# Attention feeding a max-out layer: eleven equal score groups per head pair, the attention remainder through a padded 128-row tile, a first K in two parts, and weights requested at the start in chunks

## The chip, the cores and the metric

One core of one Trainium2 chip runs the kernel. The metric is device time in microseconds (us) for one execution, of which medians over several executions are quoted. Single executions of one kernel mostly lie within 1% of each other. The profiled execution is one of them; its span (the time inside the core) is shorter than its device time by 1.7 to 1.9 us. The profiled execution of the kernel before was one of its slower ones (417.6 us).

The engines are named as in the profile: PE is the matrix engine and PEld its weight loads, ACT the scalar engine (here the exponentials), DVE the vector engine, POOL the general engine (here it sums Q and converts K and V), SP issues the transfers. Line numbers such as L412 are those of the kernel in question, so the same line has different numbers in different kernels.

## The reference

```python
# q, k, v: [8 batches, 8 heads, 1152 rows, 64], float32
q_pool = mean of each two neighbouring rows of q            # 576 rows
attn   = softmax(q_pool @ k.T / 8)                          # per batch and head
x      = (attn @ v), heads side by side                     # 4608 tokens x 512
out    = maximum(x @ w1, x @ w2) @ w_out                    # w1, w2: 512x1024, w_out: 1024x512
```

Both kernels use max(a, b) = b + relu(a - b). With `wd = w1 - w2` and `w21 = w2 @ w_out`, the output is `x @ w21 + relu(x @ wd) @ w_out`. Below, **W** is the work on PE that prepares `w21` (transposes of w2 and 32 matmuls), **H** is `relu(x @ wd)`, and **P** is the last product, in tiles of up to 128 tokens with 12 matmuls each (4 from `x @ w21`, 8 from H). H and P together are called the MoE work here.

## The kernel before

A small planner runs while the kernel is built. It keeps an estimated clock for each engine and puts every instruction into that engine's list. The lists go into the kernel in that order, with semaphores between the engines. So whatever the planner puts first is also waited for first, even where it is late on the chip.

The work goes by head pair: 32 pairs, four to a batch. For one pair PE makes score groups into three PSUM buffers (`sps`), ACT takes the exponential of each group, and PE multiplies them with V (**AV**), with a column of ones that gives the softmax sum. Everything on PE other than scores shares two PSUM accumulators (`fb`, "lanes"). When four pairs are done, the 576 tokens of a batch exist, are transposed into `xT`, and H and P can run on them. They fill the time in which PE would wait for ACT.

```python
NA, NB = 512, 64                    # 576 pooled queries = 512 + 64
# 9 score groups of 2 x 512 columns (eta), then the 64-column rests of all key tiles:
# one group of 8 rests and one of a single rest (etb)
pe_cost  = [0.22] * NT + [0.24, 0.04]
act_cost = [0.953] * (NT + 1) + [0.21]
BURST = 3                           # up to three score groups behind each other
...
def rest():                         # the AV remainder: both heads' 64 queries as one 128-row tile
    for t in range(NT):
        e.matmul(fb[m][:, 4*66:4*66+131], etb[es][:, t, :, :]..., vE[vs][:, t, :, :]...[:, 0:131], ...)
...
W_AT = (0, 1, 3)                    # w2 is requested at pair 0, w_out at pair 1, w1 at pair 3,
def w_load(part):                   # each as one transfer of 2 MB
    ...
def xtrans(b):                      # x is transposed by five DMA transposes, for every batch
    ...
# start: Q0 summed on POOL, K0 loaded in one piece and converted on DVE
load_q(0); load_k(0); cast_k(0); cast_q(0)
```

The softmax here doesn't subtract the row's maximum and nothing guards it: scores larger than these inputs give would overflow.

Of the kernel before, what the change touches and what calls it, by code (L numbers as in the profile page):

```python
# [9 lines left out]
EXP = mybir.ActivationFunctionType.Exp  # L10
ALU = mybir.AluOpType


class Plan:
# [38 lines left out]
    def op(self, eng, fn, r=(), w=(), dma=None, cost=0.1, mode="f", after=(), solo=False):  # L53
        n = len(self.ops)
        deps, raw = self.deps(r, w, after)
# [95 lines left out]
def bass_funnel_attn__then__act_maxout2_kernel(  # L151
# [14 lines left out]
    QP = 64  # L166
    QU = SQ // QP
    NA = 512
    NB = SQ - NA
    NCH = NA // P  # L170
# [5 lines left out]
    NBLK = NTOK // 512  # L176
    assert D == 64 and S == NT * P and SQ == QP * QU and QU == NT and C == H * D and E == 512
    assert NB == 64 and NTOK % 512 == 0 and NT == 9
    scale = 0.5 / float(D) ** 0.5

    ctx = ExitStack()
    with ctx:
# [10 lines left out]
        qp = [sbuf([QP, QU, 2, D], BF16, f"qp{s}") for s in range(2)]  # L193
# [4 lines left out]
        eta = [sbuf([P, 2, NT, NA], BF16, f"eta{s}") for s in range(2)]  # L198
        etb = [sbuf([P, NT, 2, NB], BF16, f"etb{s}") for s in range(2)]
        rc = [sbuf([P, 6], FP32, f"rc{s}") for s in range(2)]  # L200
# [13 lines left out]
        osb = [stage[:, NC_ * F + s * E:NC_ * F + (s + 1) * E] for s in range(3)]  # L214
# [6 lines left out]

        def setup():
            def ones(g):
                for s in range(3):
                    last = g.memset(vE[s][:, :, :, 64:66], 1.0)
                return last

            op("POOL", ones, w=["vE0", "vE1", "vE2"])
            op("POOL", lambda g: g.memset(ident[:, :], 1.0), w=["id0"])
            op("POOL", lambda g: g.affine_select(  # L230
                ident[:, :], ident[:, :], pattern=[[1, P]], compare_op=ALU.is_equal,
                fill=0.0, base=0, channel_multiplier=-1), r=["id0"], w=["ident"])

        def load_k(i):
            b, h0, s = i // NHP, 2 * (i % NHP), i % 3
            op("SP", lambda e: e.dma_start(
                kraw[s][:, :, :, :].rearrange("p h t d -> p h (t d)"),
                k[b, h0:h0 + 2, :, :].rearrange("h (p t) d -> p h (t d)", t=NT)),
                w=[f"kraw{s}"], dma=f"d_k{s}", cost=1.7)

        def load_q(i):
# [3 lines left out]
                q[b, h0:h0 + 2, :, :].rearrange("h (p r) d -> (h p) (r d)", p=QP)),  # L245
# [9 lines left out]
        def cast_k(i):  # L255
            s, r = i % 2, i % 3
            op("DVE" if i == 0 else "POOL", lambda g: g.tensor_scalar(  # L257
                kbf[s][:, :, :, :].rearrange("p t h d -> p h t d"), kraw[r][:, :, :, :],
                1.0, 1.0, ALU.mult, ALU.mult), r=[f"kraw{r}"], w=[f"kbf{s}"], cost=1.13)

        def ktrans(i):
# [4 lines left out]
                r=[f"kbf{s}"], w=[f"kT{v3}"], dma=f"d_kT{v3}", cost=1.5, mode="t")  # L266

        def cast_q(i):
            s, r = i % 2, i % 3
            for half in range(2):  # L270
                a = qraw[r][half * QP:half * QP + QP, :, :, :]
                op("POOL", lambda g, half=half, a=a: g.tensor_tensor(  # L272
                    qp[s][:, :, half, :], a[:, :, 0, :], a[:, :, 1, :], ALU.add),
                    r=[f"qraw{r}"], w=[f"qp{s}.{half}"], cost=1.4,
                    solo=half == 1)
# [16 lines left out]
        def qtrans(i):  # L292
            s = i % 2

            def go(e, m):
                mb = fb[m][:, :].bitcast(BF16)
                for u in range(QU):
                    last = e.transpose(  # L298
                        mb[:, u * QP:(u + 1) * QP],
                        qp[s][:, u, :, :].rearrange("p h d -> p (h d)"), ident[0:QP, 0:QP])  # L300
# [8 lines left out]
        def ktrans_pe(i):  # L309
# [3 lines left out]
            for lo, hi in ((0, 5), (5, NT)):  # L313
# [8 lines left out]
                def evac(m, lo=lo, hi=hi):  # L322
# [4 lines left out]
                        [f"f{m}"], [f"kT{v3}", f"f{m}"], 0.7)  # L327
                jobs.append(Job("q", [unit([f"kbf{s}", "ident"], 0.055 * (hi - lo), go)], evac,
                                ("k", i) if lo else None))
            return jobs  # L330

        def av_jobs(i):
# [4 lines left out]
            c0 = h0 * D  # L337

            def chunk(half, sb):
                def go(e, m):  # L340
                    for t in range(NT):
                        last = e.matmul(  # L342
                            fb[m][:, sb * 66:sb * 66 + 65],
                            eta[es][:, half, t, sb * P:(sb + 1) * P],
                            vE[vs][:, t, half, 0:65],
                            start=(t == 0), stop=(t == NT - 1))
                    return last
                return unit([f"eta{es}.{t}" for t in range(NT)] + [f"vE{vs}"], 0.275, go)

            def rest():  # L350
                def go(e, m):
                    for t in range(NT):
                        last = e.matmul(  # L353
                            fb[m][:, 4 * 66:4 * 66 + 131],
                            etb[es][:, t, :, :].rearrange("p h c -> p (h c)"),
                            vE[vs][:, t, :, :].rearrange("p h c -> p (h c)")[:, 0:131],
                            start=(t == 0), stop=(t == NT - 1))
                    return last
                return unit([f"etb{es}.{NT}", f"etb{es}.{NT + 1}", f"vE{vs}"], 0.53, go)

            def norm(half):
                def evac(m):
                    n = 6 if half == 0 else 4
                    c = c0 + half * D
                    a = fb[m]
                    dve(lambda e: e.reciprocal(  # L366
                        rc[half][:, 0:n],
                        a[:, 0:n * 66].rearrange("p (j c) -> p j c", c=66)[:, :, 64:65]),
                        [f"f{m}"], [f"rc{half}"], 0.13)
                    dve(lambda e: e.tensor_tensor(  # L370
                        xnat[xs][:, 0:NCH, c:c + D],
                        a[:, 0:NCH * 66].rearrange("p (j c) -> p j c", c=66)[:, :, 0:D],
                        rc[half][:, 0:NCH].unsqueeze(2).to_broadcast([P, NCH, D]),
                        ALU.mult),
                        [f"f{m}", f"rc{half}"],
                        [f"xn{xs}.{j}.{h0 + half}" for j in range(NCH)]
                        + ([f"f{m}"] if half else []), 0.38)
                    if half == 0:
                        dve(lambda e: e.tensor_scalar_mul(
                            xnat[xs][0:64, NCH, c:c + D], a[0:64, 264:264 + D],  # L380
                            rc[0][0:64, 4:5]), [f"f{m}", "rc0"], [f"xn{xs}.{NCH}.{h0}"], 0.2)
                        dve(lambda e: e.tensor_scalar_mul(  # L382
                            xnat[xs][0:64, NCH, c + D:c + 2 * D], a[64:P, 330:330 + D],
                            rc[0][64:P, 5:6]), [f"f{m}", "rc0"],
                            [f"xn{xs}.{NCH}.{h0 + 1}", f"f{m}"], 0.2)
                return evac

            last = ("x", b) if i % NHP == NHP - 1 else None
            return [
                Job("a", [chunk(0, sb) for sb in range(NCH)] + [rest()], norm(0)),  # L390
                Job("a", [chunk(1, sb) for sb in range(NCH)], norm(1), last)]
        gcount = [0]

        def scores(i, g):
# [4 lines left out]
            gcount[0] += 1  # L399

            def one(e, half, t, lo, n, col):
                h = half * 64
                return e.matmul(  # L403
# [505 lines left out]
```

## Time and profile before

| | before |
|---|---|
| device time, median | 415.4 us (414.8 to 416.0, 4 executions) |
| first exponential starts / last one ends | 13.1 / 341.7 us |
| first H matmul / first P matmul | 83.3 / 101.0 us |
| PE busy / ACT busy | 91% / 76% |

Parts 1, 2 and 4 of the page of the kernel before: busy time, the span in 40 slices of 10.4 us (tenths busy; PEclk is the granted clock of PE), and the chain of work that ended last.

```profile
PE 379.6 (91%) x4846; PEld 203.6 (49%) x4905; DVE 156.3 (38%) x355; ACT 314.4 (76%) x370; POOL 164.9 (40%) x136
PE   0787897899999999999999999999999999999996
ACT  1788997899989997999799999999999980011121
PEclk9988998999999999999999999999999999999999
PE 80%; DVE 8%; ACT 6%; issue 2%; DMA 1%; POOL 1%; another core or an unknown queue 0%
```

PE is the engine to save: it is busy nearly all the time from the ninth slice on, and it holds 80% of the chain. ACT is not full in mid-kernel; its weak stretches are at the start, and after 342 us it has almost nothing to do.

The two groups of exponentials and the two groups of AV matmuls, from the list of groups, with busy time and the mean length of one in ns; and from the list of waits (us in total, times, longest) the line for ACT.

```profile
L415 ACT ACTIVATE eta<-sps 128x1024 bf16<-128x1024 f32 x288 | 269.6, 1047 | 35.0 <-PE sps L403 34.3
L427 ACT ACTIVATE etb<-sps 128x1024 bf16<-128x1024 f32 x64 | 38.8, 673 | 0.2
L342 PE MATMUL fb<-vE,eta 128*128 128x65 bf16 x2304 | 88.7, 194 | 6.1 <-DVE xnat L382 3.1
L353 PE MATMUL fb<-vE,etb 128*128 128x131 bf16 x288 | 23.1, 226 | 0.0
ACT eta L415 <- PE sps L403: 34.3, 31, 11.1
```

A mean of 194 ns for a 65-column matmul is not what it costs PE: the records overlap (2304 of 194 ns would be 447 us, and the busy time is 88.7), and in the trace their starts are 29 ns apart.

PE's time can be split with prices that are read from such starts: 216 ns for 512 columns, 29 ns for 65, and 94 ns extra whenever a matmul on 64 rows follows one on 128 (312 ns instead of 216 to the next start) or the reverse (309 ns). What remains of the span is waiting (what matmuls take longer at a granted clock of 0.50 is in it too: there the 65-column starts are 55 ns apart).

| kernel before, us | pure PE work | changes of height | waits | waits 0 to 85 / 85 to 340 / after 340 us |
|---|---|---|---|---|
| span 415.9 | 333.8 | 321 x 0.094 = 30.2 | 51.9 | 32.6 / 10.5 / 8.7 |

So the 52 us of waits are what a better order could win, and 33 of them lie before 85 us, where the MoE work has not begun. Four lines of the timeline show what comes before it: the four subtractions `w1 - w2`, the last normalisation of the first batch's tokens, their five transposes by DMA, and the first H matmul. The columns are start, length, engine, line, operation.

```profile
63.41 6.53 DVE L488 TENSOR_TENSOR wd<-stage,xT 128x1024 bf16<-128x1024 f32 x4
70.06 0.42 DVE L370 TENSOR_TENSOR xnat<-fb,rc 128x256 bf16<-128x256 f32 x1
70.51 7.90 SPq L446 DMA_TRANSPOSE xT<-xnat  x5
83.28 0.92 PE L549 MATMUL fb<-xT,wd 128*128 128x448 bf16 x4
```

### The profile page before, as it was taken

The numbers are of one execution on the slowest core, as the hardware profiler recorded it, in microseconds if no ns is written. First come the engines' busy times: TensorE is split into PE (matmuls) and PEld (weight loads), VectorE is DVE, ScalarE is ACT, GpSimd is POOL, SyncE is SP. The second block draws the span as 40 slices with busy tenths as digits, with TensorE's granted clock in tenths as the row PEclk, the third lists the DMA queues.
The fourth block names the chain that finished last, engine by engine and source line by source line (L and its number), as shares of the span: only waits on it lengthen the run. The fifth ranks groups of instructions, "written<-read, shape, count | busy, mean of one in ns | idle before, by whom it ended". The sixth has DMA issues, their size and how long they took to land.

```text
span 415.9 us, 11123 instructions
## 1 busy us (share of the span) xinstructions
PE 379.6 (91%) x4846; PEld 203.6 (49%) x4905; DVE 156.3 (38%) x355; ACT 314.4 (76%) x370; POOL 164.9 (40%) x136
## 2 busy tenths in 40 slices
PE   0787897899999999999999999999999999999996
PEld 0355544545365536545555545555555554344442
DVE  1224738344233533244334433344333444432210
ACT  1788997899989997999799999999999980011121
POOL 5982643654346534644165536452751000000000
PEclk9988998999999999999999999999999999999999
DMA  8999997796499949974999899849964203423223
GB/s 297 403 401 391 401 283 182 155 333 159 78 344 249 277 91 315 328 225 59 303 283 240 131 307 305 267 64 325 296 138 93 46 2 65 96 50 76 64 61 66
DMA packets 81600, 85.76 MB, mean 206 GB/s; under 512 B 54416, under 2 KB 54416, under 8 KB 81552
## 3 DMA queue, kind: packets, MB, share of 16 engines
q1 hardware_dynamic: 81552, 85.05, 74.0%
q8 instruction: 38, 0.62, 0.6%
q14 instruction: 10, 0.08, 0.1%
HBM read 62.91 MB, written 9.44 MB: 174 GB/s over the span
## 4 chain that ended last, share of the span: by engine, by line
PE 80%; DVE 8%; ACT 6%; issue 2%; DMA 1%; POOL 1%; another core or an unknown queue 0%
PE fb L581 23%; PE fb L342 17%; PE sps L403 17%; PE fb L549 15%; ACT eta L415 5%; PE fb L353 4%; PE fb L298 2%; DVE wd L488 2%; PE fb L516 1%; DVE stage L598 1%; DMA qraw<-in_q_dram 1%; DVE xnat L370 1%; DVE xnat L382 1%; DVE wo L483 1%; POOL qp L272 1%
## 5 line engine op out<-in xcount | busy, mean ns | idle before, releaser
L415 ACT ACTIVATE eta<-sps 128x1024 bf16<-128x1024 f32 x288 | 269.6, 1047 | 35.0 <-PE sps L403 34.3
L272 POOL TENSOR_TENSOR qp<-qraw 64x576 bf16<-64x576 f32 x64 | 90.8, 1419 | 60.9 <-PE fb L298 54.2
L403 PE MATMUL sps<-qpT,kT 64*128 64x64 bf16 (+1 forms) x1152 | 104.6, 290 | 7.3 <-ACT eta L415 5.5
L342 PEld LDWEIGHTS fb<-vE,eta 128*128 128x128 bf16 x2304 | 79.4, 98 | 37.3 <-issue 14.4
L342 PE MATMUL fb<-vE,eta 128*128 128x65 bf16 x2304 | 88.7, 194 | 6.1 <-DVE xnat L382 3.1
L549 PE MATMUL fb<-xT,wd 128*128 128x512 bf16 (+2 forms) x304 | 76.3, 358 | 3.1 <-issue 1.3
L581 PE MATMUL fb<-wo,stage 128*128 128x512 bf16 (+1 forms) x275 | 76.5, 380 | 1.7 <-issue 1.0
L564 DVE TENSOR_SCALAR stage<-fb 128x512 bf16<-128x512 f32 (+2 forms) x68 | 44.4, 656 | 69.4 <-PE fb L549 69.0
L403 PEld LDWEIGHTS sps<-qpT,kT 64*128 64x128 bf16 x1152 | 31.2, 94 | 54.2 <-ACT eta L415 27.6
L279 POOL TENSOR_SCALAR vE<-vraw 128x1152 bf16<-128x1152 f32 x32 | 37.3, 1165 | 47.7 <-issue 35.0
L257 POOL TENSOR_SCALAR kbf<-kraw 128x1152 bf16<-128x1152 f32 x31 | 36.7, 1184 | 48.0 <-DMA kT<-kbf 47.3
L366 DVE RECIPROCAL rc<-fb 128x6 f32<-128x6 f32 x64 | 12.1, 189 | 114.0 <-PE fb L353 71.7
L549 PEld LDWEIGHTS fb<-xT,wd 128*128 128x128 bf16 x320 | 25.3, 97 | 37.2 <-DVE stage L564 6.0
L558 ACT ACTIVATE stage<-fb 128x288 bf16<-128x288 f32 (+1 forms) x12 | 5.7, 473 | 50.0 <-PE fb L549 50.0
L581 PEld LDWEIGHTS fb<-wo,stage 128*128 128x128 bf16 (+1 forms) x296 | 26.0, 98 | 30.3 <-issue 7.4
L581 PE MATMUL fb<-w,xT 128*128 128x512 bf16 (+1 forms) x130 | 37.3, 381 | 3.3 <-DVE stage L598 1.4
L427 ACT ACTIVATE etb<-sps 128x1024 bf16<-128x1024 f32 x64 | 38.8, 673 | 0.2
L598 DVE COPY stage<-fb 128x512 f32<-128x512 f32 (+1 forms) x32 | 22.1, 690 | 31.4 <-PE fb L581 31.1
L370 DVE TENSOR_TENSOR xnat<-fb,rc 128x256 bf16<-128x256 f32 x64 | 27.2, 424 | 2.2
L353 PE MATMUL fb<-vE,etb 128*128 128x131 bf16 x288 | 23.1, 226 | 0.0
L298 PE MATMUL fb<-ident,qp 64*128 64x64 bf16 x288 | 14.0, 192 | 9.8 <-POOL qp L272 8.8
L298 PEld LDWEIGHTS fb<-ident,qp 64*128 64x128 bf16 x288 | 10.7, 96 | 19.6 <-POOL qp L272 8.8
(27 smaller groups left out, 113.7 us busy)
## 6 DMA issues: line engine op xcount, KB each, us to landing
qraw<-in_q_dram SPq DMA_DIRECT2D x32, 576.0 KB, 7.0
kraw<-in_k_dram SPq DMA_DIRECT2D x32, 576.0 KB, 5.9
vraw<-in_v_dram SPq DMA_DIRECT2D x32, 576.0 KB, 8.1
out_dram<-stage SPq DMA_DIRECT2D x72, 128.0 KB, 2.5
xT<-in_moe_w_dram SPq DMA_DIRECT2D x1, 2048.0 KB, 15.6
stage<-in_moe_w_out_dram SPq DMA_DIRECT2D x1, 2048.0 KB, 19.3
stage<-in_moe_w_dram SPq DMA_DIRECT2D x1, 2048.0 KB, 17.4
xT<-xnat SPq DMA_TRANSPOSE x40, 2.5
```

The lines of the kernel that those rows point to most:

```text
L257: op("DVE" if i == 0 else "POOL", lambda g: g.tensor_scalar(kbf[s][:, :, :, :].rearrange("p t h d -> p h t d"), kraw[r][:, :, :, :], 1.0, ...
L272: op("POOL", lambda g, half=half, a=a: g.tensor_tensor(qp[s][:, :, half, :], a[:, :, 0, :], a[:, :, 1, :], ALU.add), r=[f"qraw{r}"], w=[f" ...
L279: op("POOL", lambda g: g.tensor_scalar(vE[r][:, :, :, 0:D].rearrange("p t h d -> p h t d"), vraw[r][:, :, :, :], 1.0, 1.0, ALU.mult, ALU.m ...
L298: last = e.transpose(mb[:, u * QP:(u + 1) * QP], qp[s][:, u, :, :].rearrange("p h d -> p (h d)"), ident[0:QP, 0:QP])
L342: last = e.matmul(fb[m][:, sb * 66:sb * 66 + 65], eta[es][:, half, t, sb * P:(sb + 1) * P], vE[vs][:, t, half, 0:65], start=(t == 0), stop ...
L353: last = e.matmul(fb[m][:, 4 * 66:4 * 66 + 131], etb[es][:, t, :, :].rearrange("p h c -> p (h c)"), vE[vs][:, t, :, :].rearrange("p h c -> ...
L403: return e.matmul(sps[r][:, half, col:col + n], kT[ks][h:h + 64, t, :], qpT[qs][h:h + 64, lo:lo + n], start=True, stop=True)
L415: return e.activation(eta[es][:, :, g, :], sps[r][:, :, :], EXP, scale=scale)
L427: return e.activation(etb[es][:, t0:t0 + n, :, :].rearrange("p t h c -> p h t c"), sps[r][:, :, 0:n * NB].rearrange("p h (t c) -> p h t c" ...
L549: last = e.matmul(fb[m][:, 0:size], wd[:, ct, ft * P:(ft + 1) * P], xT[:, ct, n0:n1], start=(ct == 0), stop=(ct == NC_ - 1))
L564: dve(lambda e: e.tensor_scalar_max(gT[:, ft, g0:g0 + size], fb[m][:, 0:size], 0.0), [f"f{m}"], [f"gT.{g0 // 64}.{ft}", f"f{m}"], 0.1 + si ...
L581: last = e.matmul(fb[m][0:hi - lo, :], lhs, rhs, start=(j == 0), stop=(j == NC_ + NF - 1))
```

## The change

Its intent: bring the start of the exponentials and of the MoE work forward, and make the score groups uniform so that bursts of three always fit. Cut to its core:

```diff
-    NA = 512
-    NB = SQ - NA
+    NG = 11
+    cut = [(NT * SQ * g // NG + 1) // 2 * 2 for g in range(NG + 1)]     # 11 groups of 942 +- 2 columns
...
-        eta = [... [P, 2, NT, NA] ...]; etb = [... [P, NT, 2, NB] ...]
+        et = [sbuf([P, 2 * NT * SQ + HP], BF16, f"et{s}") for s in range(2)]   # one tile, 64 zero columns behind
...
-                            eta[es][:, half, t, sb * P:(sb + 1) * P],
+                        a = (half * NT + t) * SQ + sb * P           # sb = 0..4: the fifth tile reads
+                            fb[m][:, sb * 66:sb * 66 + 65], et[es][:, a:a + P],   # 64 columns too far
-            def rest(): ...                                        # 131-column remainder
-                    if half == 0: (two more tensor_scalar_mul for the remainder)
+                        xnat[xs][:, :, c:c + D], a[:, :, 0:D], ...  # normalisation: one 128x320 operation
...
+        def xtrans_pe(b): ...           # x of the first and the last batch transposed on PE, copied by DVE
+        X_PE = (0, B - 1)
...
-            part 0: one dma_start of 2 MB per weight array; w_cast waits for the whole array
+            for c in range(NC_): dma_start of 512 KB each; each cast waits for its own chunk
...
-            if i in W_AT: w_load(W_AT.index(i)) ...                 # pairs 0, 1, 3
...
-        load_q(0)
-        load_k(0)
-        cast_k(0)                       # DVE
-        cast_q(0)                       # POOL
+        load_k(0, 0, 3)
+        load_q(0)
+        load_k(0, 3, NT)
+        cast_k0(0, 3, "kraw0.0")        # ACT
+        cast_q(0)                       # DVE
+        cast_k0(3, NT, "kraw0")         # ACT
         load_k(1); load_q(1); load_v(0); start_k(1); cast_q(1); cast_v(0)
+        start_w(0)                      # w2, in front of K2 and Q2
         load_k(2); load_q(2); load_v(1)
+        start_w(1)                      # w1
         load_k(3); load_q(3); load_v(2)
+        start_w(2)                      # w_out
```

Further: PE units are one matmul instead of two, either lane takes any job, the planner chooses by fixed ranks of the kinds of work and no longer by how far ACT is ahead, the output is 36 tiles of 128 rows instead of 37, and there are four output buffers instead of three.

## The prediction

> **What bounds it now.** TensorE. The page shows PE 91% busy against ACT 76%; the chain of waits that ended last is 80% PE. ACT does not bind in mid-kernel: its exponentials start every 904 ns back to back (timeline), which would give about 294 us for 32 head pairs; they take 329 us (13.1 to 341.7 us) and idle 34 us waiting for score matmuls (waits). After 342 us only MoE matmuls run, about 70 us.
>
> Starts of successive matmuls in the trace give a price per PE item: 216 ns for 512 columns, 29 ns for the 65-column AV matmul, 60 ns for the 131-column AV remainder, 220 ns for a score pair on two 64-row halves. Each change between 64-row and 128-row matmuls adds about 94 ns (312 instead of 216 going in). [...] At these prices the PE work is some 332 us plus 30 of changes; the other 54 us are PE waits: about 34 before 85 us (weights arrive late; the first MoE matmul is at 84.8 us), 16 in mid-kernel, 5 in the tail.
>
> **What the change does.**
> - AV remainder: 9 x 60 = 540 ns becomes 18 x 29 = 522 ns per pair. Neutral on PE. DVE normalisation falls from four operations after the first half (about 1.2 us) to two (about 0.7 us).
> - Uniform groups: same columns and the same 11 exponentials. From 1047 ns for 1024 columns and 301 for 128, 942 cost about 980, about 836 apart: 9.2 us a pair, as now. Neutral. But bursts can be three groups nearly always (now about 2.4 by my count of changes): about 250 changes instead of 320, about -6 us.
> - Output tiles: 36 of 128 rows instead of 37: 12 x 216 ns = -2.6 us. PE transposes of x for first and last batch: +2.2 us, but they replace about 6 us of DMA transposes in front of the last blocks.
> - Startup: K0's first third is loaded first, Q0 summed on DVE (estimate 1.3 to 1.9 us) instead of POOL (3.4 us), K0 cast on ACT. First exponential at about 9.5 us instead of 13.1: -3.5 us, all on the chain.
> - Weights requested at once, in chunks: landed by about 35 us (12.8 MB at the traced 400 GB/s) rather than after 60. MoE can start when batch 0 is transposed, about 58 us instead of 85. This moves PE work into idle time: early waits fall from 34 to about 20 us, 3.5 of it the startup counted above.
> - Single-matmul units, either lane for any job: mid-kernel waits 16 to perhaps 12 us.
>
> Sum: -6 -0.5 -14 -4 = about -24 us, nearly all on the chain.
>
> **Predicted 393 us**, range 383 to 405. Faster by over 2%: 0.92; within 2%: 0.07; slower: 0.01.
>
> **What would show it right.** First exponential near 9.5 us; first MoE matmul near 58 us; exponentials end near 320 to 330 us; changes of matmul height near 250; exponential duration near 980 ns; the normalisation near 0.5 us for 128x320; ACT idle behind score matmuls well below 34 us.
>
> **What would make it wrong.** Early weight traffic could delay K/Q/V of pairs 2 and 3 (DMA is saturated to 40 us), so ACT would starve. Bursts of three need three free score buffers and may leave ACT dry. Running 8 hidden-layer jobs in a row with two PSUM buffers may expose their 0.69 us DVE copy, so that tail waits grow.

The 30 us of changes are the traced 94 ns times about 320. For two numbers the traces say more than the text: two sums of 576 columns, at the 1.21 (shortest) to 1.69 us (mean) of the subtractions on DVE in the kernel before (1024 columns), make 1.36 to 1.90 us, and Q0's two, on DVE in the kernel after, took 0.75 us each (5.11 to 6.63 us); and "saturated" stands for 297 to 403 GB/s up to 42 us, with the DMA engines busy for 80% or more (the page's digits 8999).

## More of the kernel before

`wd` is ready at 69.9 us, and the tokens' transposes are issued at 70.5 to 78.4 us. Both come before H at 83.3. The two are not independent: the AV matmuls of the last tokens ended at about 64.0 us, and their normalisation stood behind the four subtractions on DVE until 69.9. So here w1 held the tokens up by about 6 us, through the order of DVE's list.

## The result

| | before | after |
|---|---|---|
| device time, median | 415.4 us (414.8 to 416.0) | 412.5 us (412.3 to 412.9) |
| ratio to before | | 0.9932 (95%: 0.9912 to 0.9952) |
| first exponential / last one ends | 13.1 / 341.7 us | 8.8 / 349.9 us |
| first H / first P matmul | 83.3 / 101.0 us | 66.2 / 85.5 us |

The kernel became 0.7% faster, which is "the same" at the 2% line. A ratio here is the mean time of one kernel's fast runs over that of the other's of the same rounds, so it is not quite the ratio of the medians quoted. The output is correct.

The page of the kernel after, the lines that answer to those of before:

```profile
PE 384.7 (94%) x5317; PEld 224.7 (55%) x5317; DVE 152.1 (37%) x308; ACT 318.9 (78%) x373; POOL 162.2 (39%) x136
PE   3887899999979999999999999999999999999895
ACT  4975899998989997999899999999999989100220
PEclk9998999999969999999999999999999999999999
PE 80%; ACT 10%; DVE 7%; DMA 2%; issue 1%; SPq 0%; POOL 0%
```

The start is fuller, but PE has a hole in the twelfth slice (113 to 123 us), where its granted clock falls too (6 in the line PEclk), and the exponentials end 8 us later than before although they began 4.4 us earlier. The groups and the wait:

```profile
L418 ACT ACTIVATE et<-sps 128x944 bf16<-128x944 f32 (+1 forms) x352 | 308.7, 963 | 32.8 <-PE sps L412 30.7
L365 PE MATMUL fb<-vE,et 128*128 128x65 bf16 x2880 | 103.4, 196 | 0.0
L377 DVE TENSOR_TENSOR xnat<-fb,rc 128x320 bf16<-128x320 f32 x64 | 31.5, 492 | 2.2
ACT et L418 <- PE sps L412: 30.7, 73, 4.4
```

ACT's exponentials cost together what they did (308.7 against 269.6 + 38.8), and so does AV in prices (85.2 us against 84.6). ACT still waits 30.7 us for scores, now in 73 waits instead of 31.

The same split of PE's time as before:

| us | pure PE work | changes | waits | 0 to 85 / 85 to 340 / after 340 |
|---|---|---|---|---|
| before, span 415.9 | 333.8 | 321: 30.2 | 51.9 | 32.6 / 10.5 / 8.7 |
| after, span 411.0 | 334.2 | 256: 24.1 | 52.7 | 26.8 / 13.9 / 11.7 |
| predicted difference | -0.5 | -6 | -18 | -14 / -4 / 0 |
| measured difference | +0.4 | -6.1 | +0.8 | -5.8 / +3.4 / +3.0 |

The work and the changes of height came out as predicted. The waits did not fall at all: 5.8 us were won before 85 us, and 6.4 us lost after it.

**Where the early gain goes.** The starts of the pairs' exponentials (us) show it, here with the first experiment beside them:

| pair | 0 | 1 | 2 | 3 | 5 | 8 | 11 | end |
|---|---|---|---|---|---|---|---|---|
| before | 13.1 | 22.3 | 33.3 | 43.9 | 64.3 | 96.8 | 129.1 | 341.7 |
| after | 8.8 | 18.9 | 35.6 | 46.6 | 66.6 | 98.4 | 131.0 | 349.9 |
| after, weights requested as before (first experiment) | 8.8 | 18.9 | 30.5 | 40.2 | 61.3 | 91.6 | 122.5 | 339.9 |

Pair 1 takes 16.7 us in the kernel after, against 11.0 before. The timeline of the kernel after in front of pair 2 shows why. The bracket is the idle time in front of the instruction and what ended it.

```profile
30.83 0.41 DVE L343 COPY kT<-fb 128x512 bf16<-128x512 bf16 x1
31.16 3.56 DVE L493 TENSOR_TENSOR wd<-stage,xT 128x1024 bf16<-128x1024 f32 x2
31.19 4.79 POOL L291 TENSOR_TENSOR qp<-qraw 64x576 bf16<-64x576 f32 x2 [5.79 <-DMA qraw<-in_q_dram]
31.37 2.64 PE L365 MATMUL fb<-vE,et 128*128 128x65 bf16 x45
34.64 0.48 DVE L343 COPY kT<-fb 128x640 bf16<-128x640 bf16 x1
35.17 0.78 PE L412 MATMUL sps<-qpT,kT 64*128 64x472 bf16 x10 [1.17 <-DVE kT L343]
35.59 1.80 ACT L418 ACTIVATE et<-sps 128x944 bf16<-128x944 f32 x2 [4.36 <-PE sps L412]
```

Read it from the bottom. ACT waits 4.36 us for scores of pair 2. PE could not make them: it had 45 AV matmuls in front of them in its list (31.37 to 34.0), and then waited 1.17 us for pair 2's transposed K. It is copied in two parts, and the part that came second is the one needed first: the copy of 640 columns holds key tiles 0 to 4, and the first score group reads tile 0, while the last four tiles had been copied at 30.83. That second copy stood on DVE behind two subtractions `w1 - w2`. One such subtraction takes 1.21 us with nothing on POOL beside it (27.59 and 29.33 us). Of these two the first takes 1.21 us (31.16 to 32.37), and POOL's sum, begun beside it (31.19 to 33.63), 2.44 instead of 1.40; the second takes 2.42 us (32.29 to 34.72), beside the rest of that sum and the start of the next. So the second subtraction is longer by 1.21 us, about the 1.26 us that the sum still ran when the first had ended, and the sum by about 1.0 us. In the kernel before, too, two of the four subtractions, beside POOL's conversions of V and K, took 2.16 us each, and the last one, alone, 1.21. What makes them longer is not shown. The planner had put 1.2 us down for each.

Two things stand beside this chain. No run puts the two K parts in order with the rest kept, so what their reversal alone costs is not shown. The other kernels with pair 2 near 36 us, experiments 14 and 18, have it too, with 4.3 and 5.0 us between the two copies; experiments 3 and 16, where the copies are reversed but start within 1 us of each other, have pair 2 at 31.1 and 31.9 us. And the granted clock is 0.50 from 31.19 to 34.60 us, so the 45 AV matmuls take 2.64 us, elsewhere in this trace 1.53. They were done before the copy, so this did not set the end of the wait.

**The second loss** is the hole at 113 us. PE and ACT in the timeline of the kernel after (lines left out in between are of the same kind):

```profile
109.94 8.64 SPq L448 DMA_TRANSPOSE xT<-xnat  x5
114.82 0.38 PE L412 MATMUL sps<-qpT,kT 64*128 64x262 bf16 x4 [0.47 <-ACT et L418]
115.67 0.38 PE L412 MATMUL sps<-qpT,kT 64*128 64x366 bf16 x4 [0.47 <-ACT et L418]
...
119.57 3.65 PE L365 MATMUL fb<-vE,et 128*128 128x65 bf16 x63
123.65 2.65 ACT L418 ACTIVATE et<-sps 128x944 bf16<-128x944 f32 x3 [2.09 <-PE sps L412]
124.77 1.37 PE L556 MATMUL fb<-xT,wd 128*128 128x512 bf16 x5
```

The MoE work of batch 0 is used up at 108 us. The next batch's tokens come late, since the attention is late, and their transposes are issued until 118.6 us. In between PE has only scores and waits 0.47 us for ACT in front of each. From 116.5 to 123.4 us (6.83 us) the granted clock is 0.50, and 63 AV matmuls take 3.65 us, elsewhere in this trace 2.08. The other stretches at 0.50 in the traces of the two kernels, the end of the kernel left out, are 3.41 us long (from 22.73, 32.97 and 70.52 us in the kernel before, from 31.19 in the kernel after), half of this one. This one begins where PE had run only 0.38 us of scores in every 0.85 us: in the 3.42 us in front of it, 113.10 to 116.52, PE was busy for 1.74. What makes the clock fall is not shown.

### The profile page after: what moved, and what is told of

Its sections match the earlier page's. It is cut to its first block, busy times and chain, and to the rows that moved or that the text cites. A ratio compares the mean times of both kernels' runs of the same rounds, so it can differ in the third digit from the quotient of the medians.

```text
span 411.0 us, 11946 instructions
## 1 busy us (share of the span) xinstructions
PE 384.7 (94%) x5317; PEld 224.7 (55%) x5317; DVE 152.1 (37%) x308; ACT 318.9 (78%) x373; POOL 162.2 (39%) x136
## 4 chain that ended last, share of the span: by engine, by line
PE 80%; ACT 10%; DVE 7%; DMA 2%; issue 1%; SPq 0%; POOL 0%
PE fb L583 24%; PE fb L365 22%; PE sps L412 17%; PE fb L556 13%; ACT et L418 9%; DMA kraw<-in_k_dram 2%; PE fb L317 2%; DVE wd L493 1%; PE fb L521 1%; DVE wo L497 1%; DVE stage L567 1%; DVE stage L597 1%; DVE xnat L377 1%; PE fb L505 1%; DVE xT L511 0%
## 5 line engine op out<-in xcount | busy, mean ns | idle before, releaser
L418 ACT ACTIVATE et<-sps 128x944 bf16<-128x944 f32 (+1 forms) x352 | 308.7, 963 | 32.8 <-PE sps L412 30.7
L291 POOL TENSOR_TENSOR qp<-qraw 64x576 bf16<-64x576 f32 x62 | 89.5, 1443 | 82.6 <-PE fb L317 67.4
L412 PE MATMUL sps<-qpT,kT 64*128 64x472 bf16 (+8 forms) x1216 | 101.8, 286 | 7.8 <-ACT et L418 5.9
L365 PEld LDWEIGHTS fb<-vE,et 128*128 128x128 bf16 x2880 | 95.6, 99 | 15.4 <-issue 8.8
L365 PE MATMUL fb<-vE,et 128*128 128x65 bf16 x2880 | 103.4, 196 | 0.0
L556 PE MATMUL fb<-xT,wd 128*128 128x512 bf16 (+3 forms) x352 | 74.8, 342 | 2.5 <-DVE stage L597 0.7
L583 PE MATMUL fb<-wo,stage 128*128 128x512 bf16 x288 | 75.1, 380 | 0.0
L567 DVE TENSOR_SCALAR stage<-fb 128x512 bf16<-128x512 f32 (+3 forms) x76 | 47.6, 627 | 36.1 <-PE fb L556 34.7
L597 DVE COPY stage<-fb 128x512 f32<-128x512 f32 x30 | 20.7, 691 | 66.6 <-PE fb L583 66.4
L583 PEld LDWEIGHTS fb<-wo,stage 128*128 128x128 bf16 x288 | 25.8, 98 | 28.7 <-issue 3.6
L583 PE MATMUL fb<-w,xT 128*128 128x512 bf16 x144 | 38.4, 380 | 1.2 <-DVE stage L567 0.4
L377 DVE TENSOR_TENSOR xnat<-fb,rc 128x320 bf16<-128x320 f32 x64 | 31.5, 492 | 2.2
L324 DVE COPY qpT<-fb 128x576 bf16<-128x576 bf16 x32 | 14.5, 453 | 20.1 <-PE fb L317 20.1
## 6 DMA issues: line engine op xcount, KB each, us to landing
xT<-in_moe_w_dram SPq DMA_DIRECT2D x4, 512.0 KB, 10.2
stage<-in_moe_w_dram SPq DMA_DIRECT2D x4, 512.0 KB, 15.5
```

Source lines behind the costliest of these rows:

```text
L291: op("DVE" if i == 0 else "POOL", lambda g, half=half, a=a: g.tensor_tensor(qp[s][:, :, half, :], a[:, :, 0, :], a[:, :, 1, :], ALU.add), ...
L365: last = e.matmul(fb[m][:, sb * 66:sb * 66 + 65], et[es][:, a:a + P], vE[vs][:, t, half, 0:65], start=(t == 0), stop=(t == NT - 1))
L377: dve(lambda e: e.tensor_tensor(xnat[xs][:, :, c:c + D], a[:, :, 0:D], rc[half][:, :].unsqueeze(2).to_broadcast([P, NCH + 1, D]), ALU.mult ...
L412: last = e.matmul(sps[r][:, h, col:col + hi - lo], kT[ks][rows(h), t, :], qpT[qs][rows(h), lo:hi], start=True, stop=True)
L418: op("ACT", lambda e: e.activation(et[es][:, 0:2 * NT * SQ].rearrange("p (h c) -> p h c", h=2)[:, :, a:z], sps[r][:, :, 0:z - a], EXP, sca ...
L556: return e.matmul(fb[m][:, 0:size], wd[:, ct, ft * P:(ft + 1) * P], xT[:, ct, n0:n1], start=(ct == 0), stop=(ct == NC_ - 1))
```

## The experiments

The theory after the result: the early request of the weights costs more than it brings, through the start of pair 2 and what follows. Rivals: the new start itself does it; bursts of three leave ACT dry; VectorE's time for the casts alone does it; the supply of MoE work binds whatever the start is. Eighteen kernels ran. Each was timed beside runs of the kernel before on the same chip; "before" took 415.9 to 417.1 us (medians) in those rounds. So a difference in us between two experiments of different rounds is good to about 1 us.

**Five of them gave NaN**: e2, e8, e11, e14, e17. Their traces have 420 weight loads for P and 70 stores of the output, all others with 36 tiles have 432 and 72: one output tile was never made. The planner's loop runs `while p_end[0] < NTOK`, and `p_end` is set by whichever tile finishes; with two lanes the last tile can finish first, and the loop then stops with the tile before it undone. The fault is in the change and stays hidden in the kernel after, where the order happens to be right. The check for races cannot see it, as nothing races. So these five are short of 12 matmuls, 12 x 216 ns = 2.6 us of PE work, and of an output copy. I quote their times as measured and add 2.6 us as an estimate of the full time.

### 1. The weights requested as before

```diff
+            if i in (0, 1, 3):
+                start_w({0: 0, 1: 2, 3: 1}[i])     # w2, w_out, w1 at pairs 0, 1, 3, as before; still in chunks
...
-        start_w(0)  /  start_w(1)  /  start_w(2)   # at the start
```

> The kernel after, but the weights (still in chunks) are asked for as the kernel before did: w2 when pair 0 starts, w_out at pair 1, w1 at pair 3. Theory A (early weights starve the early pairs, by their traffic and by their casts on DVE): pair 1's exponentials take 11 us or less instead of 16.7, the third pair starts before 30.5 us instead of 35.6, and the time falls to about 405 us, unless the first MoE matmul moves out beyond 80 us, which would eat some of it. Theory B (TensorE is full anyway, so the early loss of exponentials costs nothing): within 1.5 us of the kernel after, 411 to 414 us.

Measured: 402.35 us (402.02 to 402.85), ratio 0.9668 (0.9637 to 0.9699), correct. That is 10.2 us below the kernel after. Pair 2 starts at 30.5 us (pair 1 takes 11.6 us, a little over the 11 expected), the granted clock is 1.00 up to 340 us and falls only at the very end (mean 0.998), and the waits are 23.3 / 7.5 / 11.4 us in the three stretches, against 26.8 / 13.9 / 11.7. The exponentials of the first pairs in its timeline have no gap above 2.2 us:

```profile
8.80 2.65 ACT L418 ACTIVATE et<-sps 128x944 bf16<-128x944 f32 x3 [1.48 <-PE sps L412]
12.21 9.44 ACT L418 ACTIVATE et<-sps 128x944 bf16<-128x944 f32 x11 [0.76 <-PE sps L412]
23.79 9.44 ACT L418 ACTIVATE et<-sps 128x944 bf16<-128x944 f32 x11 [2.14 <-PE sps L412]
33.47 12.92 ACT L418 ACTIVATE et<-sps 128x944 bf16<-128x944 f32 x15 [0.24 <-PE sps L412]
```

What the early request was for did not happen either. With the weights late, the first H matmul is at 67.1 us and the first P at 82.6; with the weights early, 66.2 and 85.5. In this kernel the last subtraction for `wd` starts at 58.58 us and the copies of the first batch's tokens end at 63.6:

```profile
58.58 1.54 DVE L493 TENSOR_TENSOR wd<-stage,xT 128x1024 bf16<-128x1024 f32 x1
61.99 0.76 DVE L468 COPY xT<-fb 128x512 bf16<-128x512 bf16 x2 [0.61 <-PE fb L462]
63.32 0.28 DVE L468 COPY xT<-fb 128x256 bf16<-128x256 bf16 x1
67.08 1.02 PE L556 MATMUL fb<-xT,wd 128*128 128x512 bf16 x4
```

So `wd` is in time here too: the tokens' copies come last, and they need four pairs of attention. In the kernel after `wd` had been ready since 34.7 us, 31 us before anything used it. But the two starts of H are equal only as a net: the last normalisation of the first batch ends at 62.8 us in the kernel after and at 58.7 in this one, and H follows 3.4 and 8.4 us later. Early weights shorten the way from tokens to H by some 5 us and delay the tokens by 4. Experiment 2 shows the first without the second. The step from 83 to 67 us came from the rest of the change (chunks, casts in pieces, tokens transposed on PE), not from requesting early. These parts were not taken apart further.

### 2. All loads of the first pairs in front of the weights

```diff
         load_k(3); load_q(3); load_v(2)
+        start_w(0); start_w(1); start_w(2)        # instead of between the loads
```

> The kernel after, but all twelve weight chunks are asked for behind the loads of pairs 0 to 3: only the order of the transfers (and what follows from it) changes. Theory A by traffic: third pair starts near 29 to 30 us, first MoE matmul still before 72 us, time 403 to 407 us. Theory A by the casts on DVE alone: the third pair still starts beyond 33 us and the time stays within 2 us of 412.5. Theory B: third pair early, time still 411 to 414 us.

Measured: 404.37 us, ratio 0.9735 (0.9684 to 0.9786), NaN, so about 407 with the missing tile. Pair 2 starts at 30.4 us as expected, but pair 4 then takes 15.9 us, with ACT idle for 4.13 us. The loss has moved two pairs on and become smaller. Here the first batch's last normalisation ends at 58.3 us, as early as in experiment 1, and H starts 5.5 us earlier than there:

```profile
61.55 1.90 PE L556 MATMUL fb<-xT,wd 128*128 128x512 bf16 x8
```

So early weights do bring H forward where they do not delay the tokens; the kernel is still no faster than experiment 1, since pair 4 starves.

### 3. The casts later, the traffic unchanged

```diff
+                if entry[2] and entry[2][0] == "w" and entry[2][1] > 0 and nxt <= 2 * NG:
+                    continue              # wd and w_out casts are planned only after pair 2 has begun
```

> The kernel after with its order of transfers, but the wd subtraction and the w_out cast on DVE may not be placed before the third pair's scores have begun, so they cannot stand in front of pair 2's K copies. Theory A by casts: third pair near 30 to 31 us instead of 35.6, time 405 to 408 us. Theory A by traffic: third pair still near 33 us or later (its Q lands at 20 us and its K is cast at 25), time 410 to 413 us. Theory B: 411 to 414 us in either case.

Measured: 417.04 us, ratio 1.0025 (0.9985 to 1.0065), correct. Pair 2 starts at 31.1 us: the casts were what stood in front of it. But pairs 2, 3 and 4 take 13.0, 13.1 and 12.6 us, the granted clock falls for 10.2 us in a row (38.1 to 48.3; mean of the execution 0.978), and nothing is won. Removing one wait hands the loss to the next pairs. The waits are 56.6 us in all.

### 4. The new start alone, on the kernel before

```diff
-        load_q(0); load_k(0); cast_k(0); cast_q(0)      # kernel before
+        load_k(0, 0, 3); load_q(0); load_k(0, 3, NT)
+        cast_k0(0, 3, "kraw0.0"); cast_q(0); cast_k0(3, NT, "kraw0")   # ACT, DVE, ACT
```

> The kernel before with the new startup alone: K0 in two parts, cast on ACT, Q0 summed on DVE. First exponential near 9 us instead of 13.1. If an early start is carried to the end, the time is 411 to 412 us (4 us less than before). If TensorE has idle time later which absorbs it (MoE work must wait for whole batches anyway), it is 414 to 416 us.

Measured: 418.04 us, ratio 1.0034 (0.9997 to 1.0071), correct, and above both times that were expected. The first exponential starts at 10.95 us (about 9 expected) instead of 13.1, and pair 3 at 44.0 against 43.9: the gain is gone by then, so something else, the loads and casts as I take it, sets the pace of the first pairs there.

### 5. Bursts of two instead of three, on experiment 1

```diff
-        BURST = 3
+        BURST = 2
```

> e1_weights_as_before (402.35 us) with bursts of at most two score groups instead of three. If each change of matmul height costs the 94 ns read from the trace and TensorE binds, changes rise from about 250 to about 370 and the time by about 10 us, to 411 to 414 us. If the short idle of the exponentials behind every burst of three (0.2 to 0.4 us each) is what costs, the time falls below 400 us.

Measured: 411.94 us, ratio 0.9884 (0.9847 to 0.9920), correct: 9.6 us slower than experiment 1. PE changes height 376 times instead of 254; 122 x 94 ns = 11.5 us, the span grew by 9.8 (410.1 against 400.3), and so the waits are 1.6 us lower in the split. (The waits are what remains of the span, so the sum closes by itself; what this run adds is that 122 more changes cost 9.8 us, 80 ns each, net of that.) The attention alone becomes faster, the exponentials end at 326.0 us instead of 339.9, so bursts of three do leave ACT short, but PE pays for the changes and PE binds.

### 6. Less PE work: 256 AV matmuls left out, on experiment 1

```diff
-                    for t in range(NT):
+                    n = NT if sb < NCH else 5          # the remainder tile sums 5 of 9 key tiles
+                    for t in range(n):
```

> e1_weights_as_before with the AV remainder summed over 5 of 9 key tiles only (a wrong result on purpose): 256 of the 29 ns matmuls fewer, 7.4 us of TensorE work. If TensorE binds throughout but for the idle stretches before 85 us, where a quarter of the work lies: 396 to 397.5 us. If exponentials or the supply of MoE work bind: 401 us or more.

Measured: 402.94 us, ratio 0.9669 (0.9632 to 0.9707), wrong as intended. 7.4 us of PE work were taken away and nothing was won: the waits grew by 8.2 us, to 50.3. The timeline shows the same hole as in the kernel after, at another batch:

```profile
194.15 0.37 PE L413 MATMUL sps<-qpT,kT 64*128 64x262 bf16 x4 [0.47 <-ACT et L419]
...
197.49 2.50 PE L557 MATMUL fb<-xT,wd 128*128 128x512 bf16 x6 [0.16 <-issue]
```

MoE work comes in batches, and where it runs out, PE waits for ACT. (The lists are planned anew in this run, so part of the difference may be the new order.) "PE is 94% busy" does not say that every us taken from PE is a us won.

### 7 and 9. More accumulators at the end, on experiment 1

When the last scores are done, their three PSUM buffers are free. They become three more lanes.

```diff
+        fb += [sps[0][:, 0, :], sps[1][:, 0, :], sps[2][:, 0, :]]
...
+            if nxt == len(groups) and len(lane) == 2:
+                lane.extend([None] * 3)
# 9 only: tiles and H blocks count as done in order
-                p_end[0] = job.nb
+                p_got.add(job.nb)
+                while p_end[0] + P in p_got:
+                    p_end[0] += P
```

> e1_weights_as_before, but when the last score group is out, three of the freed score buffers serve as further accumulators. About 6 us of its TensorE waits after 340 us stand behind the copy of a hidden-layer tile out of one of the two accumulators. If the two accumulators are that cause: 396 to 398 us, and no wait above 0.15 us between hidden-layer matmuls in the tail. If DVE and ACT cannot copy faster anyway: 401 to 402.5 us.

> e7_tail_lanes (396.1 us, wrong result) with its fault mended: with five accumulators, tiles could finish out of order, and the count that frees the ring of hidden activations took the last one finished for all before it. Now it advances in order. Correct, and 395 to 398 us; if keeping order costs the gain, 400 us or more.

Measured: 7 took 396.11 us, ratio 0.9499 (0.9460 to 0.9538), but gave an error of 0.10: tiles finished out of order and the ring of H was freed too early. This is the counting fault of the NaNs in another form, and it was my addition that provoked it. 9, with the count mended, took 395.64 us (394.97 to 396.54, 6 executions), ratio 0.9504 (0.9474 to 0.9533), correct. The waits after 340 us fall from 11.4 to 4.6 us, 6.8 us, and the time from 402.35 to 395.64, 6.7 us. The tail of experiment 1, then of experiment 9, H matmuls of 256 columns:

```profile
387.39 0.77 PEld L556 LDWEIGHTS fb<-xT,wd 128*128 128x128 bf16 x8 [0.63 <-DVE stage L597]
388.51 0.77 PEld L556 LDWEIGHTS fb<-xT,wd 128*128 128x128 bf16 x8 [0.36 <-DVE stage L567]
```

```profile
375.34 1.04 PE L558 MATMUL fb<-xT,wd 128*128 128x256 bf16 x8
376.21 0.60 PE L558 MATMUL sps<-xT,wd 128*128 128x256 bf16 x4
```

With two accumulators each eight matmuls wait 0.36 us for a copy; with five the starts follow without a gap: 8 matmuls in 0.87 us (375.34 to 376.21).

### 8. Loads first, and w_out in front of w1

```diff
         load_k(3); load_q(3); load_v(2)
+        start_w(0); start_w(2); start_w(1)
```

> The kernel after with all weight chunks behind the loads of pairs 0 to 3, in the kernel before's order w2, w_out, w1 (e2 had w2, w1, w_out and gave NaN). By traffic alone pair 1's exponentials take near 11 us and the third pair starts near 30.4 us as in e2. If the weight casts on DVE then hold up a later pair, one of pairs 2 to 5 takes over 12 us and the time is 404 to 408 us; if traffic was all, every early pair takes under 11.5 us and the time is 400 to 403 us.

Measured: 408.59 us, ratio 0.9795 (0.9743 to 0.9847), NaN, so about 411. Pair 2 at 30.1 us, then pair 4 takes 14.5 and pair 9 14.3 us, with a dip of the granted clock at 114.7 to 121.5 (mean of the execution 0.981). It did not better the order of experiment 2.

### 10. w1 one pair earlier, on experiment 9

```diff
-            if i in (0, 1, 3):
-                start_w({0: 0, 1: 2, 3: 1}[i])
+            if i in (0, 1, 2):
+                start_w({0: 0, 1: 2, 2: 1}[i])
```

> e9 with w1 asked for when pair 2 starts instead of pair 3. If the first MoE matmul (67 us in e1) still waits for the weights: it moves to 63 to 65 us and the time is 1 to 3 us below e9. If the early pairs suffer from weights again: one of pairs 1 to 4 takes over 12 us and the time is 2 us or more above e9.

Measured: 402.39 us, ratio 0.9666 (0.9625 to 0.9707), correct: one pair earlier costs 6.8 us. Pair 4 takes 15.5 us. The timeline:

```profile
53.37 4.40 DVE L495 TENSOR_TENSOR wd<-stage,xT 128x1024 bf16<-128x1024 f32 x2
58.45 2.35 PE L367 MATMUL fb<-vE,et 128*128 128x65 bf16 x45 [2.49 <-DVE xnat L379]
61.78 1.80 ACT L420 ACTIVATE et<-sps 128x944 bf16<-128x944 f32 x2 [3.54 <-PE sps L414]
```

Two subtractions take 4.40 us here (2.06 and 2.42 us, with POOL's sums beside them), the normalisation of an AV tile stands behind them on DVE, PE waits 2.49 us for that, and ACT then 3.54 us for scores. This is the same chain as in front of pair 2 of the kernel after, at another place.

### 11. The old start, on experiment 1

```diff
-        load_k(0, 0, 3); load_q(0); load_k(0, 3, NT)
-        cast_k0(...); cast_q(0) on DVE; cast_k0(...)
+        load_q(0); load_k(0); cast_k(0); cast_q(0)      # DVE and POOL, as before
```

> e1_weights_as_before with the kernel before's startup: Q0 then K0 whole, K0 cast on DVE, Q0 summed on POOL. First exponential near 13 us instead of 8.8. If the early start is carried to the end once no early pair starves: 405.5 to 407 us, 4 us above e1's 402.35. If it is absorbed, as e4 was in the kernel before: within 1.5 us of e1.

Measured: 406.04 us, ratio 0.9748 (0.9707 to 0.9789), NaN, so about 408.6: 3.7 us slower than experiment 1 as measured, about 6 with the missing tile. The first exponential starts at 11.4 instead of 8.8 us. But pair 4 also takes 13.7 us here, against 10.8 in experiment 1, so the loss is not the later start (2.6 us) alone, and the two are not separated. That the new start gains where it is not followed by a starved pair, which experiment 4 alone would not have told, is likely, but its size stays open.

### 12. The early weights, on the kernel before

```diff
-            if i in W_AT: ...                            # pairs 0, 1, 3
+        start_w(0)   # in front of load_k(2)
+        start_w(2)   # in front of load_k(3)
+        start_w(1)   # behind load_v(2)
```

> The kernel before, with its weights asked for as the change does: w2 behind V0, w1 behind V1, w_out behind V2 (each still in one transfer). If early weights starve the early pairs in this kernel too: one of pairs 1 to 3 takes over 13 us and the time is 416 to 422 us. If they only let the MoE matmuls start sooner: first one near 73 us instead of 83 and the time is 410 to 414 us.

Measured: 422.15 us, ratio 1.0164 (1.0110 to 1.0218), correct: 1.6% slower than before. The first H comes at 73.9 us instead of 83.3, so here the weights do bring the MoE work forward, and still the kernel loses: pairs 0, 2 and 9 take 13.6, 13.5 and 13.8 us, and the waits rise from 51.9 to 56.4 us. The cost of the early request does not need the rest of the change.

### 13. The kernel after with short casts

```diff
-                    wd[:, ct, :], w1f[:, ct, :], w2f[:, ct, :], ALU.subtract)
+                    wd[:, ct, 0:64], w1f[:, ct, 0:64], w2f[:, ct, 0:64], ALU.subtract)    # 1/16; w_out likewise
+            op("DVE", lambda e: (e.memset(wd[:, :, :], 0.01), e.memset(wo[:, :, :], 0.01))[1], ...)   # fill
```

> The kernel after with exactly its instruction order on every engine, but the four wd subtractions and the four w_out casts touch a sixteenth of their columns (the rest is filled with a constant at the start: a wrong result on purpose). Traffic is unchanged. If the time that these eight operations hold DVE, in front of pair 2's K copies, starves the early pairs: third pair near 31 us instead of 35.6, no wait of PE for MoE near 113 us is left or it is shorter, time 404 to 408 us. If the early traffic does it: third pair beyond 34 us, time 411 to 413 us.

Measured: 417.56 us, ratio 1.0029 (0.9988 to 1.0071), wrong as intended. The fill at the start was my mistake: it held the first exponential back by 5.0 us (13.8). From the first exponential to pair 2 it takes 26.2 us, against 26.8 in the kernel after and 21.7 in experiment 1. So making these casts short, with the order of all lists kept, wins only 0.6 us of the 5: now pair 1 is late as well (15.2 us for it), PE waits 2.27 us for a conversion of w2 in front of pair 1's scores (ACT idle 3.43 us), and the 45 AV matmuls still stand in front of pair 2 (2.01 us). So in the old order short casts do not bring pair 2 forward, which speaks for the order of the lists as the cause. It is not a clean test, since the fill moved everything behind it by 5 us against the loads.

### 14 and 15. The planner told of longer casts

```diff
-                    [f"w1f{ct}", f"w2f{ct}"], [f"wd{ct}", "w2f"], 1.2)
+                    [f"w1f{ct}", f"w2f{ct}"], [f"wd{ct}", "w2f"], 2.0)        # w_out: 0.6 -> 1.5
```

> The kernel after with two numbers of its planner changed: a wd subtraction is planned with 2.0 us instead of 1.2, a w_out cast with 1.5 instead of 0.6 (the trace has 1.2 to 1.8 and 0.7 to 1.5). Result unchanged, the order is planned anew. If mis-set planner costs put the casts where they block: third pair before 32.5 us and 404 to 409 us. If it is the lump of DVE work as such: a later pair pays, as in e3, and the time is 410 to 417 us.

> e9_tail_lanes_in_order with the same two planner numbers. Its weight casts stand behind pairs 1 to 5 and hold nothing up, so little should change: within 1.5 us of e9's 395.6; below 393 us if its pair 4 (10.8 us) was still held up by casts.

Measured: 14 (on the kernel after) took 406.28 us, ratio 0.9757 (0.9716 to 0.9798), NaN, so about 409: some 3.7 us won. Pair 2 is still late (36.2 us, under 32.5 expected), so the time fell as expected and the reason given for it did not hold. (The expectation's 1.2 to 1.8 and 0.7 to 1.5 us are means of merged records; single ones in the kernel after are 1.21 to 2.42 and 0.68 to 1.89.) But H of batch 1 starts at 114.0 instead of 124.8 us, the granted clock does not dip there (mean of the execution 0.996), and the waits from 85 to 340 us fall from 13.9 to 8.1. So the second loss does not follow by necessity from the first. 15 (on experiment 9) took 396.83 us, ratio 0.9529 (0.9501 to 0.9558), correct, no better than 9 itself. Experiment 9's in-order count is in it, and no tile is missing.

### 16 and 17. One array moved at a time

```diff
# 16: only w1 late
-        start_w(1)                     # in front of K3
+        start_w(2)                     # w_out takes its place
-        start_w(2)
+            if i == 3: start_w(1)      # w1 at pair 3
# 17: only w2 later
-        start_w(0)                     # in front of K2, Q2
+        start_w(0)                     # behind V1, in front of w1
```

> The kernel after, with one array moved: w2 is still requested in front of pair 2's K and Q, w_out takes the place that w1 had (in front of pair 3), and w1 is requested at pair 3. If the loss of 10 us (after 412.5, all three late 402.4) comes from the subtractions w1 - w2 on VectorE being planned in front of pair 2, this gives 402 to 404, with pair 2 starting at 30 to 32 us. If it comes from w2's 2 MB standing in front of K2 and Q2, pair 2 still starts at 34 to 36 us and the time is 409 to 413.

> The kernel after, with one array moved: w2 is requested behind K2, Q2 and V1, directly in front of w1; everything else stays. If w2 in front of K2 and Q2 is the cause, pair 2 starts at 30 to 32 us and the time falls to 402 to 405. If the subtractions are the cause, they only move a little, a later pair is delayed instead, and the time stays at 408 to 413.

Measured: 16 took 409.89 us, ratio 0.9842 (0.9795 to 0.9889), correct. 17 took 406.17 us, ratio 0.9758 (0.9709 to 0.9807), NaN, so about 409. Both expectations are half right: either move brings pair 2 to 31.9 and 30.8 us, so the delay in front of pair 2 goes when either is moved, w2's traffic in front of K2 and Q2 or the subtractions that w1 allows. (Each move also gives new lists, in which the two K copies follow each other sooner, 0.9 us in 16 and 1.6 us in 17.) And both moves pay most of it back later: in 16 pair 5 takes 13.7 us, in 17 pair 4 takes 14.9. In 16 the subtractions now stand between the transposes of the first tokens and their copies:

```profile
57.54 1.80 DVE L493 TENSOR_TENSOR wd<-stage,xT 128x1024 bf16<-128x1024 f32 x1
59.26 0.74 DVE L468 COPY xT<-fb 128x512 bf16<-128x512 bf16 x2
59.72 0.73 PE L462 MATMUL fb<-ident,xnat 128*128 128x128 bf16 x8 [1.12 <-DVE xT L468]
65.87 2.65 ACT L418 ACTIVATE et<-sps 128x940 bf16<-128x940 f32 x3 [2.27 <-PE sps L412]
```

The granted clock is 0.50 from 61.4 to 68.2 us in that run, too (five H matmuls of 512 columns take 2.32 us at 63.00, in the kernel after 1.37 at 124.77). So no single array, cast or wait carries the 10 us.

### 18. The kernel after with five accumulators at the end

```diff
# the edit of experiment 9, with the weights still requested early
```

> The kernel after with the five accumulators at the end and nothing else changed (weights early). If the loss at the start and the loss at the end are independent, it gains what it gained with late weights, 402.4 to 395.6, so 405 to 407.5 against 412.5. If the two share a cause (the MoE work is already shifted), it gains under 3 us: 410 or more.

Measured: 404.89 us (403.09 to 408.42), ratio 0.9716 (0.9660 to 0.9772), correct: 7.6 us below the kernel after, where experiment 9 is 6.7 below experiment 1. So the gain at the end is about the same with early and with late weights, and the two losses add, as far as the spread of this run's executions (5.3 us) can tell.

## Why the prediction was wrong, point by point

The prediction said 393 us with a range of 383 to 405; measured were 412.5. Its sum had four terms.

- **Changes of height, -6 us: right.** 256 changes (predicted about 250) save 6.1 us, and experiment 5 bought 122 of them back for 9.6 us.
- **PE work, about -0.5 us: right within 1 us.** It rose by 0.4.
- **"Weights landed by about 35 us ... MoE can start when batch 0 is transposed, about 58 us instead of 85 ... early waits fall from 34 to about 20 us", -14 us: this step failed.** It took the early request as free for the attention. The weights did land and `wd` was ready at 34.7 us, but the first batch's tokens were normalised only at 62.8 us, as pair 2 had been held up, and H began at 66.2. With the weights late (experiment 1) the tokens are there at 58.7 and H begins at 67.1. What the early request brought was therefore about 1 us of H, net, and what it cost was 10.2 us (412.5 against 402.35). Early waits fell by 5.8 us to 26.8, not to 20; with the weights late they fall to 23.3.
- **Mid-kernel waits "16 to perhaps 12 us", -4 us: failed in sign.** The first value was itself too high; by the finer count they were 10.5 us, and rose to 13.9. Experiment 1 has 7.5 there, so the term was right for the rest of the change and was spent by the early weights (the hole at 113 us).
- **Tail, no term: +3.0 us.** It was named as a risk ("eight hidden-layer jobs in a row with two PSUM buffers"), with no number. Experiment 9 shows 6.8 us in that place.

Of its signs: the first exponential (predicted 9.5, measured 8.8 us), the exponential's length (980 and 963 ns) and the normalisation (0.5 and 0.492 us) were right. The end of the exponentials (320 to 330, measured 349.9), the first MoE matmul (58, measured 66.2) and ACT's idle time ("well below 34", measured 30.7) were wrong. For the exponential's length the two traced lengths of the kernel before, 301 ns for 128 columns and 1047 for 1024, give about 979 ns for 942 columns on a straight line, as predicted; the trace has 963, and the measurement decides.

The risk "early weight traffic could delay K/Q/V of pairs 2 and 3 so ACT would starve" was named, and put into the 7% for "within 2%". It was the main event. The prediction had treated the waits before 85 us as waits for weights. They were in the main waits for tokens, and the tokens come from the attention, which the weights' traffic and casts disturb; in the kernel before, too, w1's subtractions held the last tokens up by about 6 us.

What is shown: that requesting early costs 10 us in this kernel, that it brings H no earlier there on balance, that it costs this through late score groups and not through extra work (pure work and changes are equal in experiment 1 and the kernel after: 334.3 and 334.2, 23.9 and 24.1 us), and that pair 2 is in time again when the traffic or the casts are moved and the lists planned anew. Read off the trace, but not separated by a run, is which part of that chain weighs most: the subtractions in front of the K copy, the reversed order of the two K parts, or the AV matmuls in front of the scores. What also stays open: why the order with w2 at pair 0, w_out at pair 1 and w1 at pair 3 hands the loss on to no later pair, while six others (experiments 2, 3, 8, 10, 16, 17) do; with the old start (experiment 11) it does so as well. With a fixed order of lists, each setting gives another order, and the runs do not tell which rule would find the good one.

The fastest kernel is experiment 9: 395.6 us, 5.0% under the kernel before and about 4% under the kernel after.

## What to carry to other kernels

Before moving a load forward, ask what its first user waits for last: if that is something else, the load only stands in the way of what that something needs. In a kernel with fixed instruction lists, a cast that comes in early is planned in early, and every engine behind it waits in order (here the K copy at 34.64 us behind 3.56 us of subtractions), so the place of a cast needs a plan of its own, and its arrival should not set it. Which place is right is not shown: moved a little later (experiment 3) the casts cost as much, and in the kernel before, four in a row just before their first use held the tokens up by about 6 us. And a loop that ends on "the last one is done" must count in order when work can finish out of order: a changed schedule showed a missing output tile that the tested schedule had hidden.
